# Another written order of all work, other engines for sums, scalings and divisions, and s and b loaded later, in a fused attention and two-layer MLP kernel

## The chip, the cores and the metric

One Trainium2 chip, one core. The time is in device microseconds (us) for one execution of the program. A run gives one time; the number compared is the median of several. The engines are PE (TensorE, matrix products), DVE (VectorE) and ACT (ScalarE), both elementwise, POOL (GpSimd, elementwise, works on SBUF alone) and SP (SyncE), which here only issues the DMA transfers. Each engine takes its instructions in order; DMA transfers are issued by SP in order too.

## What is computed

Windowed attention over 4 batches, 8 heads, 576 positions and head size 64, then two MLPs on the 2304 x 512 result, each 512 to 2048 to 512.

```python
scores = scale * q @ k.T                     # per head; scale = 1/8
scores = where((rel >= 0) & (rel < 128), scores - slope[h] * |rel|, -1e9)
attn = exp(scores - max); attn = attn / (sum(attn) + 1e-9)
x = (attn @ v) laid out as 2304 x 512
x = (s * relu(x @ w_in1)**2 + b) @ w_out1    # first MLP
out = relu(x @ w_in2)**2 @ w_out2            # second MLP
```

The MLP weights are fp64 words in memory.

## The kernel before

Every fp32 operand of the MLP products is split into a rounded half and the rest (hi and lo), and each product is made of three matmuls (hi by hi, hi by lo, lo by hi). A split is a copy on ScalarE (hi) followed by a subtraction on VectorE (lo) that waits for it. The fp64 weight words are turned to fp32 by a first stage (ScalarE scales the low words, VectorE merges), a second stage (a scaling, a shift on VectorE, an addition on GpSimd) and a split. Weights of the later parts are halved ahead of time, stored to DRAM and loaded again. Products of the later parts are made by seven instead of eight block products, for which sums and differences of weight blocks and of operands are made first.

All work is written out by hand as one order: the string `ORDER` (line 38 on) holds 2463 tokens, and line 1212 runs through it, each token calling one piece that issues instructions on one or more engines. The wrapper `InOrder` (line 19) keeps each engine's instructions in that order, SP's too. So the order of tokens is the order on every engine, and an instruction that waits holds up what is behind it on its own engine only. At most eight transfers are open at a time, since each takes one of eight semaphores in turn.

Tokens that matter here, k counting attention units, weight pieces or steps:

- `Dk`, `Sk`, `Pk`, `Tk`, `Ck`, `Uk`, `Xk` (lines 358 and 467): an attention unit's load, scores, probabilities (score, max and exp), divisions with transposes, copies out of PSUM, output products and their split into x (or, for the last blocks, a store to DRAM). Units 32 to 39 are the short blocks at the end of each batch (`tail_unit`, tiles with _t). `UNIT_ENGINES` says for units 0 to 31, six letters each, on which engine (s ScalarE, v VectorE) four divisions and two copies run.
- `lgi`, `agi`, `bgi`, `cgi` (line 278): load, first stage, second stage and split of piece i of weight group g of the first MLP. `PIECE_ENGINES` gives the engine of the scaling in b and of the subtraction in c.
- `Ln`, `Gn`, `Hn`, `Mn` (line 548): first product, relu and scaled square (needs s), shifted halves (needs b), second product of step n of the first MLP on attention blocks.
- `i` (line 711): loads s and b, each spread over the partitions, by two DMAs.
- `nk.i` (line 734): sums of first-MLP weight blocks, on GpSimd; `fk.i` their split and store; `kk.i` other stores.
- `lk.r`, `ak.r`, `bk.r`, `ck.i`, `dk.i`, `xk.r`, `yk.r`, `Sk.0`, `Sk.1`, `Nk.0`, `Nk.1`: the same for the second MLP's weights. `S` (line 864) makes sums of w_in2 blocks on VectorE, `N` (line 899) of w_out2 blocks on GpSimd, `R` and `t` split and store those.
- `wk.i` loads the weights of step k, `Yn.q` an input block, `Vn.m` and `Tn.i` split it and make its differences; `pk.m` are the first products of step k, `mk`, `uk`, `vk` copies out of PSUM, `jk.c`, `rk.c`, `hk.c` sum with relu, square and halves, `Fk.j` the second products.
- In the last two blocks `en.e` loads, `gn.e` makes the operand of, and `Xn.e` is second product e; `C` and `O` bring results out.

Of the kernel before, what the change touches and what calls it, by code (L numbers as in the profile page):

```python
# [15 lines left out]
P = 128  # L16


class InOrder:
# [19 lines left out]
    D0 S0 D3 D1 S3 l00 P0 S1 l02 P3 T0 i l03 P1 T3 T1 a02 C0 a00 U0 a03 b02 b00 D4 D2 S2 X0 D5 C1 P2 U1 S4 C3 P4 T2 T4  # L39
    U3 D6 l01 a01 c00 C2 U2 c02 b01 X3 X1 S5 X2 D7 L0 b03 l10 P5 L1 C4 T5 c01 G0 G1 c03 a10 L2 l12 L3 a12 l11 H0 C5 U4  # L40
    b10 H1 U5 G2 X4 X5 G3 a11 H2 c10 D8 b12 M0 M1 S7 S6 M2 l13 L4 L5 b11 H3 P7 P6 M3 T7 D9 T6 c11 C7 C6 l20 G4 U7 U6 L6
    G5 a13 H4 X6 c12 l22 G6 H5 L7 S8 M4 b13 P8 G7 X7 H6 M5 H7 L8 L9 T8 G8 L10 D10 l21 c13 G9 C8 U8 a20 H8 X8 a22 M6 L11
    S9 M7 G10 L12 M8 H9 b20 l23 P9 T9 G11 H10 b22 L13 H11 C9 U9 M9 D11 G12 G13 M10 X9 S10 L14 D12 M11 a21 a23 D13 H12
    L15 b21 P10 T10 M12 G14 H13 c21 c20 C10 M13 H14 U10 L16 G15 c22 l30 b23 X10 H15 G16 L17 l32 S11 L18 G17 L19 M14 M15
    P11 T11 H16 H17 c23 G18 a30 C11 k0.0 l31 G19 L20 U11 H18 k2.1 a32 X11 H19 G20 M16 S12 L21 M17 b30 M18 P12 T12 l33
    a31 G21 c30 M19 H20 C12 b31 U12 X12 L22 S13 a33 G22 L23 P13 M20 L24 T13 H21 b32 C13 H22 G23 c31 H23 G24 l34 M21 U13
    M22 c32 b33 H24 D14 l35 L25 X13 a34 G25 L26 G26 L27 c33 S14 L28 H25 H26 k5.0 D15 M23 M24 b34 P14 T14 G27 M25 C14 a35
    c34 U14 L29 b35 X14 G28 H27 H28 c35 L30 S15 G29 D16 k4.0 M26 P15 M27 M28 T15 C15 L31 H29 D17 G30 H30 U15 X15 M29 S16
# [112 lines left out]
def attention_mlp2_kernel(ctx, tc, first0, first1, qkv0, qkv1, qkvt, w_in1, w_out1, s_in, b_in, w_in2, w_out2, out):  # L165
# [1089 lines left out]
```

## Time and profile before

| | us |
|---|---|
| median of 3 runs | 930.66 |
| lowest run | 930.6 |
| the profiled execution, its own time | 926.7 |
| its span in the profile | 924.9 |
| PE busy in the span | 883.8 (96%) |
| DVE busy | 659.2 (71%) |
| ACT busy | 545.0 (59%) |
| POOL busy | 175.5 (19%) |

One run of the three took 2689.89 us; the median leaves it aside. Busy is the time in which an engine has an instruction at work. A PE instruction's end is modelled, since matmuls overlap, so PE busy is not PE at its peak. PEclk in the views is the clock that TensorE was granted, as a share of full speed. All lines of the kernel read L29, the wrapper, so instructions are told apart by tile names: `out<-in`. The tiles s, u are attention's PSUM banks, ha and oa the first MLP's, px, py, po and q the later products'; names that begin with m2 are places of later weights and operands, st the staging of weight words, sph and spl the weight sums and their halves, ywoh, ywol, yr and the like the results of squares in the last two blocks.

### The profile page before, as it was taken

The numbers are of one execution on the slowest core, as the hardware profiler recorded it, in microseconds if no ns is written. First come the engines' busy times: TensorE is split into PE (matmuls) and PEld (weight loads), VectorE is DVE, ScalarE is ACT, GpSimd is POOL, SyncE is SP. The second block draws the span as 40 slices with busy tenths as digits, with TensorE's granted clock in tenths as the row PEclk, the third lists the DMA queues.
The fourth block names the chain that finished last, engine by engine and source line by source line (L and its number), as shares of the span: only waits on it lengthen the run. The fifth ranks groups of instructions, "written<-read, shape, count | busy, mean of one in ns | idle before, by whom it ended". The sixth has DMA issues, their size and how long they took to land.

```text
span 924.9 us, 16342 instructions
## 1 busy us (share of the span) xinstructions
PE 883.8 (96%) x5680; PEld 790.0 (85%) x5680; DVE 659.2 (71%) x1471; ACT 545.0 (59%) x1242; POOL 175.5 (19%) x259
## 2 busy tenths in 40 slices
PE   5799999999999999889999999999999889999997
PEld 4689999877777787669999998888999879999987
DVE  6998886454446788756455876898858968648675
ACT  6988886444556578645444565766656535446442
POOL 3342231000026373300010012222243400000000
PEclk8999999999999999999999999999999999999999
DMA  8456525542229788979957958769899887867772
GB/s 317 168 158 178 185 90 171 160 140 65 75 63 307 245 274 269 316 279 358 313 192 263 365 178 283 267 214 318 306 342 339 306 289 254 267 258 239 245 241 80
DMA packets 131378, 216.83 MB, mean 234 GB/s; under 512 B 15840, under 2 KB 74208, under 8 KB 131296
## 3 DMA queue, kind: packets, MB, share of 16 engines
q1 hardware_dynamic: 131296, 215.79, 69.5%
q8 instruction: 45, 0.74, 0.3%
q14 instruction: 37, 0.30, 0.1%
HBM read 146.02 MB, written 69.73 MB: 233 GB/s over the span
## 4 chain that ended last, share of the span: by engine, by line
PE 75%; DMA 9%; DVE 6%; ACT 4%; issue 4%; POOL 2%; SPq 1%; ACTq 0%; DVEq 0%; POOLq 0%
PE px L29 13%; PE po L29 13%; PE oa L29 12%; PE ha L29 12%; PE py L29 10%; PE q L29 9%; PE s L29 6%; DMA m2wol<-wd 2%; POOL st L29 2%; PE u L29 1%; DMA st<-w_in 1%; SPq L29 1%; DMA raw<-first 1%; DMA xd<-raw_t 1%; DMA raw_t<-qkvt 1%
## 5 line engine op out<-in xcount | busy, mean ns | idle before, releaser
L29 POOL TENSOR_TENSOR st<-st 128x256 int32<-128x256 int32 (+1 forms) x120 | 83.9, 720 | 362.0 <-DVE st L29 297.2
L29 ACT ACTIVATE pr<-pr,nd 128x256 f32<-128x256 f32 (+1 forms) x129 | 59.5, 474 | 46.6 <-DVE nd L29 46.6
L29 ACT ACTIVATE st<-st 128x512 int32<-128x512 uint32 (+3 forms) x84 | 69.4, 840 | 4.9 <-DMA st<-w_out 3.0
L29 DVE SCALAR_TENSOR_TENSOR r_all<-r_all,s_sb 128x256 f32<-128x256 f32 (+1 forms) x64 | 42.2, 664 | 27.6 <-ACT r_all L29 27.5
L29 ACT ACTIVATE tr<-tr 128x384 f32<-128x384 f32 x48 | 25.3, 526 | 55.9 <-DVE tr L29 55.9
L29 PE MATMUL oa<-ga,woh 128*128 128x256 f32 x256 | 48.6, 289 | 0.0
L29 ACT ACTIVATE r_all<-ha 128x256 f32<-128x256 f32 (+1 forms) x64 | 30.7, 483 | 28.1 <-PE ha L29 26.3
L29 POOL TENSOR_TENSOR sph<-wih,wil 128x256 f32<-128x256 f32 x32 | 23.9, 772 | 121.3 <-PE ha L29 121.2
L29 DVE SCALAR_TENSOR_TENSOR st<-st 128x512 int32<-128x512 int32 (+1 forms) x42 | 38.0, 911 | 6.1 <-ACT st L29 5.7
L29 PEld LDWEIGHTS oa<-ga,woh 128*128 128x128 f32 x256 | 39.7, 191 | 2.8 <-issue 1.7
L29 DVE CUSTOM_DVE_ANT_0 pr<-s,bases 128x256 f32<-128x256 f32 (+1 forms) x96 | 31.7, 386 | 8.5 <-PE s L29 8.5
L29 PE MATMUL ha<-x0h,wih 128*128 128x256 f32 x128 | 37.6, 294 | 0.0
L29 PE MATMUL ha<-x0h,wil 128*128 128x256 f32 x128 | 36.3, 283 | 0.5 <-DVE wil L29 0.5
L29 PE MATMUL ha<-x0l,wih 128*128 128x256 f32 x128 | 36.2, 283 | 0.0
L29 PE MATMUL oa<-ga,wol 128*128 128x256 f32 x128 | 36.2, 283 | 0.0
L29 POOL TENSOR_TENSOR sph<-sph 128x256 f32<-128x256 f32 x32 | 27.1, 864 | 28.2 <-DVE spl L29 27.4
L29 PE MATMUL s<-raw 64*128 64x256 f32 (+1 forms) x224 | 29.6, 384 | 1.8 <-issue 1.8
L29 ACT ACTIVATE r_all<-px 128x384 f32<-128x384 f32 x32 | 15.6, 489 | 24.4 <-PE px L29 24.4
L29 PE MATMUL px<-m2xl,m2wil 128*128 128x384 f32 x138 | 27.8, 335 | 0.0
L29 DVE TENSOR_SCALAR st<-st 128x512 int32<-128x512 int32 (+1 forms) x42 | 22.8, 543 | 6.6 <-ACT st L29 6.1
L29 PEld LDWEIGHTS ha<-x0h,wih 128*128 128x128 f32 x128 | 24.4, 191 | 2.7 <-issue 2.0
L29 POOL TENSOR_TENSOR st<-st,st 128x256 f32<-128x256 f32 x24 | 22.3, 954 | 23.3 <-DMA st<-wx 20.9
(678 smaller groups left out, 2772.3 us busy)
## 6 DMA issues: line engine op xcount, KB each, us to landing
m2wih<-wd SPq DMA_DIRECT2D x19, 512.0 KB, 5.1
st<-w_in SPq DMA_DIRECT2D x8, 1024.0 KB, 6.6
st<-w_out SPq DMA_DIRECT2D x16, 512.0 KB, 4.6
ws<-spl SPq DMA_DIRECT2D x16, 512.0 KB, 5.4
m2wih<-ws SPq DMA_DIRECT2D x16, 512.0 KB, 6.7
wd<-m2wol SPq DMA_DIRECT2D x14, 512.0 KB, 5.7
m2wol<-we SPq DMA_DIRECT2D x26, 256.0 KB, 4.8
st<-w_out SPq DMA_DIRECT2D x6, 1024.0 KB, 7.2
```

The lines of the kernel that those rows point to most:

```text
L29: ins = op(*args, **kw)
```

## The change

`ORDER` has the same tokens in another sequence. Its beginning before and after:

```diff
-    D0 S0 D3 D1 S3 l00 P0 S1 l02 P3 T0 i l03 P1 T3 T1 a02 C0 a00 U0 a03 b02 b00 D4 D2 S2 X0 D5 C1 P2 U1 S4 C3 P4 T2 T4
-    U3 D6 l01 a01 c00 C2 U2 c02 b01 X3 X1 S5 X2 D7 L0 b03 l10 P5 L1 C4 T5 c01 G0 G1 c03 a10 L2 l12 L3 a12 l11 H0 C5 U4
+    D0 S0 D3 P0 S3 D1 l00 l02 P3 S1 T0 P1 T3 T1 a00 D4 D2 l03 C0 a02 b00 U0 X0 b02 S2 S4 C1 U1 C3 U3 P2 P4 T2 l01 D5 D6
+    T4 a03 a01 c00 b03 b01 C2 U2 D7 X1 S5 c02 X2 X3 L0 i l10 P5 L1 C4 T5 G0 c01 a10 C5 G1 U4 L2 c03 H0 b10 U5 l12 H1 L3
...
```

The end of the first MLP and the start of the second:

```diff
-    n7.3 T38 c1.3 n7.4 G61 w1.0 L62 d1.3 C38 X36 P39 U38 T39 w2.4 n7.5 w2.0 X38 c1.4 U37 x1.2 d1.4 H61 X37 c1.5 G62 C39
-    d1.5 M60 U39 L63 X39 Q Y0.0 M61 Y0.1 Y0.3 Y0.2 f7.0 w0.0 w0.1 H62 w0.3 G63 f7.1 M62 w1.1 V0.1 T0.1 H63 T0.3 M63 T0.2
...
+    c1.3 d1.3 X36 G61 C38 L62 U38 P39 w2.0 T39 x1.3 c1.4 x1.2 X38 n7.2 n7.3 H61 U37 M60 d1.4 C39 c1.5 X37 U39 d1.5 G62
+    X39 Q Y0.0 Y0.1 L63 n7.4 Y0.3 n7.5 M61 w0.0 Y0.2 w0.1 f7.1 H62 f7.0 G63 M62 V0.1 T0.1 H63 T0.2 w0.4 V0.5 M63 E40
...
```

Part of the second products of block 2:

```diff
-    p22.7 p22.5 e2.2 X2.0 v22 j22.1 y6.4 p22.3 j23.0 T3.2 r22.1 t4.2 N5.1 R5.2 X2.1 r23.0 R5.3 y6.5 N6.0 V3.1 p22.4 X2.2
-    R6.0 t4.3 p23.6 e2.5 V3.2 p23.5 R6.1 g2.6 g2.8 V3.6 t5.1 g2.7 j22.2 j22.3 r22.2 e2.3 X2.3 e2.4 r21.2 u23 r22.3 y7.4
-    X2.4 t5.0 g2.9 g2.10 X2.5 e2.7 N6.1 g2.11 p23.7 y7.5 R6.3 e2.10 v23 j23.1 e2.6 X2.6 t5.3 T3.4 r23.1 R6.2 r21.3 e2.9
...
+    R5.3 g2.6 g2.5 e2.9 g2.8 T3.4 X2.4 X2.5 X2.6 r22.3 V3.6 t6.1 g2.9 y7.5 g2.7 g2.10 N6.1 R6.3 g2.11 y7.4 w23.3 u23
+    g2.12 p23.7 N7.0 t6.0 v23 t5.0 t5.2 t5.3 e2.10 e2.13 j23.1 X2.7 X2.8 N7.1 r23.1 R7.2 p23.4 X2.9 R7.3 e2.11 g2.14
...
+    r23.3 g2.19 O2.2.2 g2.20 t6.3 O2.2.0 g2.21 X2.16 X2.17 X2.18 g2.24 X2.19 g2.22 t7.0 X2.20 g2.25 g2.26 X2.21 e2.27
+    e2.31 p24.2 m24 g2.27 g2.23 e2.35 X2.24 X2.25 X2.26 e2.23 X2.22 X2.27 g2.28 e2.30 e2.28 e2.40 e2.39 p24.6 g2.32
...
```

`UNIT_ENGINES` has other letters: 32 instead of 34 of the 128 divisions and 39 instead of 41 of the 64 copies are ScalarE's. A table by token, read by two helpers, chooses engines of the sums, of the scalings in b and of one subtraction in c; s and b become the two columns of one tile.

```diff
+CHOICE = dict(x.split(":") for x in """
+    N1.1:v N2.1:v N3.0:v N3.1:v N7.1:v S0.1:g S1.1:g S2.0:g S3.0:g S3.1:g S4.0:g b0.0:vg b2.2:vg b3.0:vg b3.1:vg
+    b33:vg b34:vg b4.1:vg b4.3:vg b5.2:vg b7.0:vg b7.2:vg c35:g n0.1:v n0.2:v n1.0:v n1.2:v n1.3:v n2.2:v n2.3:v
+    n3.1:v n4.3:v n4.5:v n5.1:v n5.4:v n6.1:v n6.2:v n7.1:v n7.2:v n7.3:v n7.5:v
+""".split())
...
-    s_sb = const.tile([P, 1], F32, tag="s_sb", name="s_sb")
-    b_sb = const.tile([P, 1], F32, tag="b_sb", name="b_sb")
+    sb = const.tile([P, 2], F32, tag="s_sb", name="s_sb")
+    s_sb, b_sb = sb[:, 0:1], sb[:, 1:2]
...
+    now = [""]
+
+    def choice(n, usual):
+        return CHOICE[now[0]][n] if now[0] in CHOICE else usual
+
+    def adder(usual):
+        return vector if choice(0, usual) == "v" else gpsimd
...
-        if engine == "s":
+        if choice(0, engine) == "s":
             scalar.activation(h, h, AF.Copy, scale=2.0 ** -112)
...
-        t, tt = pool_sum[0].bitcast(F32), gpsimd.tensor_tensor
+        t, tt = pool_sum[0].bitcast(F32), adder("g").tensor_tensor
...
-        (l0, l1, h0, h1), tt = quarters(k), vector.tensor_tensor
+        (l0, l1, h0, h1), tt = quarters(k), adder("v").tensor_tensor
...
-        lo, hi, tt = slice(0, BLK), slice(BLK, DM), gpsimd.tensor_tensor
+        lo, hi, tt = slice(0, BLK), slice(BLK, DM), adder("g").tensor_tensor
...
-    run(table[x] for x in ORDER.split())
+    for x in ORDER.split():
+        now[0] = x
+        table[x]()
```

Of the chosen tokens, `n` with a last digit under 4 makes one addition, with 4 or 5 two; `N` and `S` make two each; each `b` scales 128x512 words.

## Rows read from the trace of the kernel before

**Rows 1.** Page, busy us with share of the span and instructions.
```profile
PE 883.8 (96%) x5680; PEld 790.0 (85%) x5680; DVE 659.2 (71%) x1471; ACT 545.0 (59%) x1242; POOL 175.5 (19%) x259
```

**Rows 2.** Busy time by stretch: length, PE, PEld, DVE, ACT, POOL; PEclk; DMA share; GB/s.
```profile
0.00:75.00 75.00, 57.65 (x463) 49.01 (x464) 61.50 (x179) 60.49 (x142) 25.85 (x51) 0.93 0.64 220
75.00:350.00 275.00, 274.37 (x1846) 229.34 (x1846) 181.85 (x500) 171.75 (x437) 68.79 (x98) 1.00 0.51 161
350.00:400.00 50.00, 45.58 (x315) 35.70 (x316) 39.01 (x113) 36.60 (x98) 16.60 (x30) 1.00 0.89 293
400.00:425.00 25.00, 21.21 (x103) 18.41 (x102) 16.14 (x21) 11.97 (x22) 0.00 (x0) 0.93 0.87 305
425.00:700.00 275.00, 274.57 (x1471) 252.57 (x1471) 197.57 (x347) 159.22 (x320) 48.46 (x65) 1.00 0.81 282
700.00:775.00 75.00, 68.04 (x465) 64.68 (x465) 63.01 (x116) 36.67 (x83) 15.84 (x15) 1.00 0.85 287
775.00:850.00 75.00, 75.00 (x500) 75.00 (x499) 47.78 (x93) 39.36 (x83) 0.00 (x0) 1.00 0.79 273
850.00:924.90 74.90, 67.37 (x527) 65.24 (x525) 52.37 (x105) 28.93 (x62) 0.00 (x0) 1.00 0.60 189
```

**Rows 3.** Waits of PE, whole span: us in total, times, longest.
```profile
PE s L29 <- DMA rwih<-first: 4.2, 1, 4.2
PE s L29 <- DVE f_3woh L29: 4.0, 3, 2.2
PE s_t L29 <- DVE pr_t L29: 3.2, 5, 1.1
PE px L29 <- ACT tu L29: 2.7, 2, 2.1
PE q L29 <- DMA m2wol<-we: 1.4, 1, 1.4
```

**Rows 4.** Timeline of POOL and DVE, 728 to 768: start, us, operation, [idle before].
```profile
729.96 2.74 POOL L29 TENSOR_TENSOR st<-st,st 128x256 f32<-128x256 f32 x3 [1.74 <-DMA st<-wx]
...
731.02 1.08 DVE L29 TENSOR_TENSOR ywol<-ywol 128x384 f32<-128x384 f32 x1
...
736.92 0.55 DVE L29 TENSOR_TENSOR ywol<-ywol 128x384 f32<-128x384 f32 x1
```

**Rows 5.** The head: ACT's wait (5 to 35), then timeline rows of SP and PE.
```profile
ACT st L29 <- DMA st<-w_out: 2.5, 2, 1.8
...
3.15 0.47 SPq L29 DMA_DIRECT2D s_sb<-s_in  x1
...
19.48 1.65 PE L29 MATMUL s<-rwil 64*128 64x128 f32 x8 [3.17 <-DMA rwil<-first]
```

**Rows 6.** Timeline around 405: ACT, then PE.
```profile
404.85 0.84 ACT L29 ACTIVATE m2xh<-yf 128x768 fp32r<-128x768 f32 x1 [4.09 <-DMA yf<-xd]
...
406.36 0.49 PE L29 MATMUL oa<-ga_63h,woh 128*128 128x512 f32 x1 [1.31 <-ACT ga_63h L29]
408.75 0.50 PE L29 MATMUL oa<-ga_63l,woh 128*128 128x512 f32 x1 [1.90 <-DVE ga_63l L29]
```

**Rows 7.** Timeline of DVE and PE at 752, and DVE's last instruction.
```profile
752.66 0.56 DVE L29 TENSOR_TENSOR m2wih<-ywih,m2wih 128x384 fp32r<-128x384 f32 x1 [0.67 <-ACT m2wih L29]
...
752.68 1.69 PE L29 MATMUL q<-m2xl,m2wih 128*128 128x256 f32 x9 [1.09 <-ACT m2wih L29]
...
920.92 0.42 DVE L29 TENSOR_TENSOR ob<-q,k3u 128x256 f32<-128x256 f32 x1 [1.29 <-PE q L29]
```

**Rows 8.** Groups by shape, whole span: count, busy us, mean ns, idle before.
```profile
L29 POOL TENSOR_TENSOR sph<-wih,wil 128x256 f32<-128x256 f32 x32 | 23.9, 772 | 121.3 <-PE ha L29 121.2
...
L29 DVE TENSOR_TENSOR st<-st,st 128x256 f32<-128x256 f32 x12 | 5.4, 460 | 0.5
...
L29 ACT ACTIVATE st<-st 128x512 f32<-128x512 f32 x28 | 18.9, 674 | 1.5 <-DVE st L29 1.3
...
L29 DVE TENSOR_SCALAR st<-st 128x512 int32<-128x512 int32 x28 | 12.5, 445 | 5.1 <-ACT st L29 4.7
```

More of the change, by code (lines that the diff above doesn't have):

```diff
@@ L44 @@
[L44 to L48, printed above, removed]
@@ new lines @@
+    C11 G17 l32 a30 G18 U11 H17 X11 H18 L19 G19 b30 L20 S12 M16 L21 k0.1 a32 l31 M17 M18 P12 T12 a31 H19 G20 c30 C12 H20
+    L22 l33 G21 b32 U12 X12 L23 G22 H21 S13 L24 M19 a33 b31 M20 M21 H22 P13 l34 b33 T13 G23 C13 c31 a34 M22 H23 U13 L25
+    c33 G24 G25 c32 L26 k3.0 D14 L27 H24 M23 H25 X13 D15 S14 G26 G27 M24 l35 b34 L28 L29 P14 k4.1 T14 M25 H26 a35 C14
+    H27 c34 k4.0 G29 b35 U14 M26 D16 X14 G28 H28 S15 L30 c35 P15 M27 M28 T15 C15 D17 G30 L31 H29 G31 U15 X15 L32 S16 M29
+    H30 H31 D18 G32 L33 P16 T16 M30 D19 C16 H32 G33 M31 M32 H33 S17 U16 L34 P17 T17 X16 G34 C17 M33 L35 H34 S18 U17 M34
@@ new lines @@
+    F15.7 t0.0 R0.2 p17.2 F15.2 V2.3 F15.10 R0.3 t0.3 u16 t0.2 V2.5 p16.7 O1.1 y1.4 O1.4 v16 F15.8 y1.5 p17.1 w20.0
+    j16.0 F14.0 T2.4 p16.5 N1.0 V2.4 p16.4 Y3.0 m17 j17.0 j16.1 p16.3 r16.0 w19.2 j16.2 j16.3 r16.3 p17.5 y2.4 w19.1
+    p17.6 R1.0 N1.1 u17 F14.6 R1.1 p18.2 r17.0 y2.5 R1.2 t1.1 T3.1 t1.2 N2.0 p17.7 t1.0 F15.0 v17 j17.1 p18.1 m18 R1.3
+    p17.3 j17.3 w20.2 w20.1 t1.3 p18.6 O1.2 p17.4 u18 j18.0 w19.3 j17.2 N2.1 R2.1 p18.5 p18.7 R2.0 p19.1 v18 y3.4 t2.0
+    p18.4 r17.1 r17.3 R2.2 p19.2 R2.3 m19 y3.5 j18.1 j18.2 g2.0 w21.0 r18.0 p18.3 F15.6 p19.6 t2.2 j19.0 w20.3 j18.3
@@ new lines @@
+    e2.25 e2.19 C2.1.1 r23.2 g2.16 e2.20 e2.26 C2.1.0 e2.29 j23.3 X2.14 g2.17 e2.22 e2.21 g2.15 g2.18 X2.15 e2.24 p24.1
+    r23.3 g2.19 O2.2.2 g2.20 t6.3 O2.2.0 g2.21 X2.16 X2.17 X2.18 g2.24 X2.19 g2.22 t7.0 X2.20 g2.25 g2.26 X2.21 e2.27
+    e2.31 p24.2 m24 g2.27 g2.23 e2.35 X2.24 X2.25 X2.26 e2.23 X2.22 X2.27 g2.28 e2.30 e2.28 e2.40 e2.39 p24.6 g2.32
+    e2.32 X2.23 g2.33 C2.7.0 e2.33 X2.28 g2.29 X2.32 e2.36 g2.34 X2.33 X2.29 g2.30 e2.34 X2.34 g2.35 C2.7.1 e2.38 g2.31
+    X2.30 e2.47 w27.0 e2.37 e2.44 X2.35 e2.42 e2.43 X2.31 g2.36 e2.41 g2.40 g2.41 g2.37 g2.39 e2.46 X2.36 X2.40 C2.6.0
@@ new lines @@
+    X2.37 g2.38 e2.54 V3.4 u24 C2.6.1 e2.45 X2.38 e2.51 X2.39 X2.41 e2.49 g2.43 g2.46 g2.42 V3.7 g2.45 e2.48 O2.5.0
+    g2.44 X2.42 X2.43 X2.44 g2.47 X2.45 O2.5.2 p24.7 X2.46 g2.48 e2.53 V3.5 w25.0 v24 e2.50 X2.47 e2.52 g2.49 p24.4
+    w25.1 j24.0 p24.5 g2.50 O2.4.2 O2.4.0 X2.48 X2.49 g2.51 V3.3 w25.2 p25.1 j24.1 X2.50 X2.51 p24.3 e3.13 e2.55 p25.2
+    w26.0 j24.2 m25 w25.3 p25.6 w26.3 w27.1 g2.53 g2.52 X2.52 j24.3 u25 j25.0 w26.1 p25.5 p25.7 v25 X2.53 w26.2 w28.0
+    p26.1 j25.1 p25.4 p25.3 j25.2 w27.2 w28.1 p26.2 p27.1 w27.3 m26 j25.3 w28.2 w29.0 e3.12 g2.55 j26.0 p27.2 p26.6
@@ new lines @@
+    r29.2 j30.1 e3.1 r29.1 p31.2 w31.2 r30.0 r24.3 p30.3 m31 r28.3 j31.0 X3.0 e3.4 e3.3 p31.6 p30.4 j30.3 r30.1 r27.2
+    r30.3 g3.3 e3.8 e3.5 r29.3 e3.6 X3.1 r31.0 X3.2 u31 g3.10 g3.7 p31.7 p31.5 g3.6 e3.14 X3.3 X3.4 X3.5 e3.16 g3.12
+    e3.9 g3.11 v31 X3.6 p31.4 r26.1 e3.7 g3.8 e3.19 j30.2 j31.1 r30.2 e3.20 e3.52 X3.7 e3.15 X3.8 e3.18 e3.49 p31.3
+    r31.1 g3.13 e3.21 g3.14 g3.16 g3.9 X3.9 X3.10 X3.11 e3.17 g3.17 e3.22 j31.2 X3.12 r31.2 C3.1.0 g3.18 e3.50 g3.15
+    e3.26 C3.1.1 e3.23 g3.19 j31.3 X3.16 X3.17 X3.13 e3.24 g3.20 r31.3 e3.25 g3.27 X3.14 X3.18 X3.15 g3.24 g3.25 g3.21
@@ L267, in second_stage @@
         na, nw = words.shape[1:3]
-        da, dw = max(1, 2 * P // nw), min(nw, 2 * P)
+        eng, most = (gpsimd, 2 * P) if choice(1, "g") == "g" else (vector, DM)
+        da, dw = max(1, most // nw), min(nw, most)
         for i in range(0, na, da):
@@ L271, in second_stage @@
                 y = (slice(None), slice(i, i + da), slice(c, c + dw))
[L272 removed]
+                eng.tensor_tensor(to[y], h32[y], l32[y], ALU.add)
     last_load = []
@@ L308, in third @@
                 part = (slice(None), slice(n, n + step)) if k else (slice(None), slice(None), slice(n * P, (n + step) * P))
-                split(hi[part], lo[part], words()[..., 0].bitcast(F32), act_copy, pool_sub if how[1] == "g" else dve_sub)
+                split(hi[part], lo[part], words()[..., 0].bitcast(F32), act_copy, pool_sub if choice(0, how[1]) == "g" else dve_sub)
             how = PIECE_ENGINES[g][i]
@@ L541, in scaled_square @@
     def scaled_square(r):
[L542 removed]
+        vector.scalar_tensor_tensor(r, r, s_sb, r, ALU.mult, ALU.mult)
     def shifted_halves(hi, lo, r):
[L545 to L546 removed]
+        scalar.activation(hi, r, AF.Identity, bias=b_sb)
+        vector.scalar_tensor_tensor(lo, r, b_sb, hi.bitcast(F32), ALU.add, ALU.subtract)
     def step_of(n, d, f, lo, w, start, stop):
```

179 lines of the change are left out of this document (78 added, 101 removed).

## Prediction, made before the change was run

> **What bounds the kernel now.** I read the line of busy times first, then the busy time by stage, then TensorE's waits, and last the timelines of three places where TensorE stands still. The span is 924.9 us and TensorE is busy for 883.8 of it [rows 1]. So a change that leaves TensorE's work as it is, as this one does, has 41.1 us to win from. The stages [rows 2] say where: idle is the stretch less PE busy. It is 17.4 us in 0 to 75, 4.4 in 350 to 400, 3.8 in 400 to 425, 7.0 in 700 to 775 and 7.5 in 850 to the end. It is only 0.6 in 75 to 350, 0.4 in 425 to 700 and nothing in 775 to 850. In those last three stages (625 us) TensorE is the bound, and whatever VectorE, ScalarE and GpSimd do sooner there is not seen. Of the 41.1 some can't go: the first matmul stands for 4.2 us before its input has landed [rows 3], and about 4 us lie between the last eviction's start at 920.92, just behind the last matmul, and the end of the span [rows 7]. So some 33 us are open to an order, in four places.
>
> TensorE's own waits [rows 3] name VectorE and ScalarE more than DMA: three waits on f_3woh in the attention at the head, five on pr_t in the short attention blocks, two on tu, one on a loaded weight.
>
> **VectorE and GpSimd block each other.** The same VectorE subtraction of 128x384 takes 0.55 us at 736.92, with GpSimd idle, and 1.08 at 731.02, while three GpSimd sums run from 729.96 and take 2.74 together [rows 4]. The operation that comes second waits for the other's end. A consequence for this change: taking turns in the written order moves a wait from inside an instruction to in front of it. It makes the port no freer. Time comes back only where the delayed instruction was the one that TensorE stood for. The Trainium skill (SBUF — State Buffer, section Who interferes with whom) has a rule that speaks against a gain: a VectorE instruction with two SBUF inputs and a GpSimd instruction that reads SBUF exclude each other for the whole instruction, whoever starts first, so another sequence of the same pairs frees nothing. By that rule alone the term of 700 to 775 below would be 0 and the sum 926.7. The two rows agree with the exclusion; that the sequence can't matter to TensorE they do not show, so the term is made from the waits there.
>
> **The change, part by part.** The written order holds the same 2463 tokens; only their sequence differs, and each engine and the DMA queue follow it.
>
> *Engines of the sums.* 21 additions of the `n` tokens and 10 of the `N` tokens go from GpSimd to VectorE, 12 of the `S` tokens the other way. On GpSimd one takes 0.772 us, on VectorE 0.460 [rows 8]. VectorE: +31 x 0.46 - 12 x 0.46 = +8.7 us. GpSimd: -31 x 0.772 + 12 x 0.772 = -14.7. The piece of c35 goes to GpSimd (two additions, +1.5; about 0.7 less on VectorE). 11 scalings go from ScalarE, 0.674 each, to VectorE, 0.445 [rows 8]: -7.4 and +4.9. Of the divisions and evictions two each change to VectorE net, within 2 us. In all VectorE gets 13 to 15 us more, GpSimd 13 less, ScalarE some 8 less. VectorE has 93 us free of 275 in 75 to 350 (busy 181.85) and 77 of 275 in 425 to 700 [rows 2], where TensorE covers it: 0. In 350 to 400, where VectorE is busy for 39.0 of 50, about ten of the `n` sums land (4.6 us). Room is left, and the same sums stop blocking VectorE from GpSimd, so I put 0, with 2.5 either way. If that cover were gone, the price would be those 4.6.
>
> *s and b loaded later.* Their two loads, the first of them issued at 3.15, take about 0.47 us of issue each [rows 5], ahead of l03 and of the attention inputs. They go behind L0, where only G0 needs them, a product of 12 matmuls later. With them l03 (by the code 256 rows of 1024 words, 1 MB) is moved behind two attention inputs (D4 and D2, 0.5 and 0.4 MB), and l01 ahead of D5 and D6. D2 is what S2 stood 3.17 us for at 19.48 [rows 5]. By the 220 GB/s of 0 to 75 [rows 2] a megabyte takes 4.8 us, so D2 can come early enough for S2 not to wait for it. l03 comes later by D4 and D2, 0.9 MB or some 4 us, but its reader (a03) is moved behind two rounds of probabilities and T2.
>
> *The head.* ScalarE is what fills up there: it is busy 60.5 of 75, VectorE 61.5 [rows 2]. It waits 2.5 us for w_out [rows 5], because a02 and a03 stand ahead of work whose inputs are there. In the new order a00 comes first, whose words landed earlier, and a03 stands late, so these 2.5 can go. Of TensorE's waits at S2 and T2 (3.2 and up to 4.0 in three) more is named, but the same ScalarE work still stands ahead of L0. Hence I take the 2.5 and 0.5 of the small waits: **-3.0**. Bounds: -5.0 (S2's wait and half of the others gone) and +1.0 (l03 late for b03 and c03). TensorE is full from 75 on, so what is won here stays.
>
> *The switch of stages, 400 to 425.* ScalarE waits 4.09 us for a load of attention output (V0.1) at 404.85 and only then makes ga_63h, for which TensorE stands 1.31; VectorE then does V0.1 and T0.1 before ga_63l, for which TensorE stands 1.90 [rows 6]. In the new order V0.1 and T0.1 still precede H63, and TensorE still has L63, M61, M62 between U39 and M63. The wait must return: **0**, bounds -3 and +3. The granted clock is 0.93 here [rows 2], a mean of its two levels (2.4 and 1.2 GHz) right after those waits; that would return too.
>
> *700 to 775.* TensorE is idle 7.0 and VectorE busy for 63.0 of 75, GpSimd 15.8 [rows 2]. This is where blocking costs. The `N` sums that remain on GpSimd (N6, N7.0) sit among operands that TensorE needs; N7.1 moves to VectorE. Behind it, operands for the second products come singly, VectorE, then ScalarE, then VectorE again: at 752.66 VectorE waits 0.67 for ScalarE, and TensorE 1.09 [rows 7]. The new order lets p24.2 and p24.6 come sooner among these products and covers some of that. The wait on tu (2.1 of the 2.7) and half of the 1.09-type waits make **-3.0**. Bounds: -7.0, all idle gone; +3.0, if u23, now behind more operand copies on ScalarE, comes later still.
>
> *775 to the end.* Nothing of GpSimd is left there. 7.5 us idle less 4 after the last matmul leave 3.5; the order of operands alone differs: **-1.0**, from -3 to +2.
>
> Sum: -3.0 + 0 + 0 - 3.0 - 1.0 = -7.0. The profiled execution took 926.7 us around its span of 924.9, so 919.7; the median of the runs is 930.66, 4.0 above it, so **923.7 us**.
>
> **The rivals.**
> *Given back.* The head's 3 us vanish because VectorE and ScalarE are near full at 25 to 75, and in 700 to 775 transfers, at 0.85 of the DMA engines [rows 2], set the pace. For: PE waits on a DMA there [rows 3]. Against: most of those waits name ScalarE and VectorE. Time: 930.7 less 0 to 4, so 927 to 931.
> *Slower, by loads that come late.* One place: 425 to 700, where the DMA share is 0.81 [rows 2] and idle is 0.4 us only because each of about 16 steps (1471 matmuls, some 90 a step by the code) finds its weights. SP issues in order; a load placed behind a store whose VectorE half is late starts late. Price: one wait like the longest on a weight, 1.4 [rows 3], once or twice a step, 22 to 45 us, so 946 to 968. It outweighs the 7 us from five such waits on. Against: the loads of a step stand well ahead of its products in both orders.
> *Much faster, by the port.* If most of the 33 us hang on blocked instructions, the head's idle but for the first load (17.4 - 4.2 = 13.2) and the 7.0 of 700 to 775 go: 930.7 - 20.2 = 910.5. Against: at the head TensorE's longest waits are for loads, not for a blocked instruction [rows 3, 5].
>
> **How the numbers follow.** Forecast 0.55 (912 to 927), given back 0.25 (927 to 936 with its upper bounds), late loads 0.08 (of it 0.05 above 949.3), much faster 0.12 (below 912). About 2%, or 18.6 us, is what a measurement of this kernel can tell from no change: faster than 912.0 has 0.12, slower than 949.3 has 0.05, between them 0.83. The range 911 to 936 leaves out some 0.08 above and 0.12 below.
>
> **What would show it.** Right: S2 without its wait and the first product, L0, some 3 us sooner; both waits at M63 and the lowered clock still there; TensorE idle in the stretch that answers 700 to 775 near 4; VectorE busy some 13 us more less what blocking it lost. Wrong: waits on weights in the full stretches, or TensorE's idle total above 41.

## The result, and the profile after

The new kernel took 916.6 us in the median of four runs (914.44 to 919.35), against 930.63 for the kernel before beside it: a ratio of 0.986, 95% interval 0.983 to 0.988. A second measurement of it (below, e9) gave 917.81 against 928.77, 0.988 (0.986 to 0.990). The forecast was 923.7 with a range of 911 to 936, so the time lies inside the range, 7 us on the quick side of the forecast, and within the 2% that I gave 0.83. The profiled execution took 916.5 us (span 914.7), where that of before took 926.7.

First the page's line of busy times, to be read beside [rows 1]:

```profile
PE 878.5 (96%) x5680; PEld 787.4 (86%) x5680; DVE 663.4 (73%) x1504; ACT 536.7 (59%) x1227; POOL 167.7 (18%) x242
```

TensorE idles 914.7 - 878.5 = 36.2 us, before 41.1. Of the 10.2 us between the spans 4.9 are therefore idle time; 5.3 are busy time of the same 5680 matmuls. About half of these the granted clock explains (mean 0.996 instead of 0.993, 0.3% of 884 us); the rest I leave open, since a matmul's end is modelled. VectorE is busy 4.2 us more, ScalarE 8.3 less, GpSimd 7.8 less; I had forecast 13 more, 8 less and 13 less, and what became of the rest was not traced. The same stretches as in [rows 2], with the same columns:

```profile
0.00:75.00 75.00, 58.40 (x490) 50.08 (x492) 65.03 (x186) 63.25 (x146) 27.08 (x51) 0.95 0.69 237
75.00:350.00 275.00, 274.56 (x1855) 229.51 (x1854) 187.89 (x523) 170.36 (x442) 62.23 (x88) 1.00 0.51 162
350.00:400.00 50.00, 46.71 (x306) 36.74 (x304) 38.16 (x111) 32.87 (x86) 15.76 (x25) 1.00 0.87 280
400.00:425.00 25.00, 23.04 (x127) 20.97 (x128) 18.91 (x29) 14.44 (x26) 0.00 (x0) 1.00 0.89 325
425.00:700.00 275.00, 273.59 (x1466) 252.21 (x1465) 200.19 (x357) 155.03 (x314) 53.12 (x68) 1.00 0.82 288
700.00:775.00 75.00, 69.93 (x503) 67.20 (x502) 62.50 (x120) 41.52 (x92) 9.51 (x10) 1.00 0.85 288
```

The kernels stand at different work at the same time, so stretches of time can mislead when a kernel is 10 us ahead. For that reason I made a ledger by work. All kernels have the same matmuls. I gave each one the spacing at which matmuls of its shape follow each other undisturbed (229 ns for 128x512 and so on; 841 us in all) and read off when each kernel has done the same amount. A stage is then the time between two such marks; in the new kernel the marks 35, 300, 345, 360, 500, 550, 650 and 690 lie near 61, 341, 392, 412, 552, 604, 707 and 752 us. Each line is one profiled execution.

| us | to 35 (head) | 35-300 | 300-345 (short attention blocks) | 345-360 (switch) | 500-550 | 650-690 | all other | end |
|---|---|---|---|---|---|---|---|---|
| before | 64.6 | 280.5 | 54.1 | 21.1 | 51.1 | 49.2 | 399.8 | 920.5 |
| before, again (e5) | 66.9 | 280.6 | 53.9 | 21.0 | 51.1 | 49.3 | 399.9 | 922.6 |
| new | 61.4 | 279.8 | 51.2 | 19.6 | 51.7 | 45.1 | 401.5 | 910.3 |
| new, again (e9) | 61.4 | 279.8 | 51.1 | 19.0 | 51.8 | 45.3 | 400.8 | 909.1 |
| new order, old engines (e1) | 63.1 | 281.5 | 52.3 | 18.8 | 54.8 | 46.0 | 402.4 | 918.8 |
| old order, new engines (e2) | 69.5 | 284.8 | 53.5 | 22.3 | 52.5 | 49.3 | 402.2 | 934.1 |
| old units (e6) | 62.8 | 281.3 | 51.2 | 19.1 | 53.3 | 46.5 | 401.0 | 915.2 |
| old sums (e7) | 61.1 | 279.8 | 52.6 | 18.5 | 54.3 | 47.4 | 400.9 | 914.7 |

By means of the two pairs, 11.8 us went: 4.3 at the head, 0.7 in 35 to 300, 2.9 in the short attention blocks, 1.8 at the switch of stages, 4.1 in 650 to 690; 0.6 came back in 500 to 550 and 1.3 elsewhere, most of it behind 690. Outside the head and the switch, two executions of one kernel agree within 0.25 us in each named stage. Only 500 to 550 is less certain: the new kernel's order gives 51.7 there in four executions, but 52.9 and 52.6 in two variants (e8, e12) that differ from it elsewhere. And the mark 690 stands among waits of TensorE, so what lies on either side of it moves by a microsecond with the spacings taken: from 650 to the end together about 3 us went.

TensorE's waits, whole span, beside [rows 3] (us in total, times, longest):

```profile
PE s L29 <- ACT f_3woh L29: 4.5, 2, 2.8
PE s L29 <- DMA rwih<-first: 4.2, 1, 4.2
PE s L29 <- ACT f_3wol L29: 3.8, 1, 3.8
PE q L29 <- ACT m2woh L29: 2.3, 2, 1.5
PE oa L29 <- DVE ga_63l L29: 2.3, 1, 2.3
...
PE s_t L29 <- DVE pr_t L29: 1.7, 4, 0.7
...
PE px L29 <- ACT tr L29: 0.6, 1, 0.6
PE px L29 <- ACT tu L29: 0.6, 1, 0.6
```

S2's wait for rwil is gone (0.8 in e9), pr_t costs 1.7 instead of 3.2, tu 0.6 instead of 2.7. Two waits at the head took new names (f_3woh and f_3wol, both for ScalarE). At the switch one of the two waits of [rows 6] is left:

```profile
396.45 0.85 ACT L29 ACTIVATE m2xh<-yf 128x768 fp32r<-128x768 f32 x1 [2.98 <-DMA yf<-xd]
397.20 0.71 ACT L29 ACTIVATE ga_63h<-r_all,s_sb 128x512 fp32r<-128x512 f32 x1
...
400.81 0.50 PE L29 MATMUL oa<-ga_63l,woh 128*128 128x512 f32 x1 [2.30 <-DVE ga_63l L29]
```

ScalarE still stands for the load with ga_63h behind it, but 1.1 us less, and ga_63h is there when TensorE comes at 398.12.

### The profile page after: what moved, and what is told of

The parts are those of the page before. It is cut to its first block, busy times and chain, and to the rows that moved or that the text cites. A ratio compares the mean times of both kernels' runs of the same rounds, so it can differ in the third digit from the quotient of the medians.

```text
span 914.7 us, 16299 instructions
## 1 busy us (share of the span) xinstructions
PE 878.5 (96%) x5680; PEld 787.4 (86%) x5680; DVE 663.4 (73%) x1504; ACT 536.7 (59%) x1227; POOL 167.7 (18%) x242
## 4 chain that ended last, share of the span: by engine, by line
PE 81%; DVE 9%; ACT 4%; DMA 3%; issue 2%; SPq 1%; POOL 0%; ACTq 0%; DVEq 0%
PE ha L29 14%; PE po L29 14%; PE px L29 13%; PE oa L29 12%; PE py L29 10%; PE q L29 8%; PE s L29 7%; PE u L29 2%; DMA m2wol<-wd 1%; DVE ywoh L29 1%; DVE st L29 1%; DVE m2woh L29 1%; DVE pr_t L29 1%; DMA yf<-xd 1%; DMA st<-w_out 1%
## 5 line engine op out<-in xcount | busy, mean ns | idle before, releaser
L29 POOL TENSOR_TENSOR st<-st 128x256 int32<-128x256 int32 (+1 forms) x123 | 87.2, 729 | 363.8 <-DVE st L29 251.0
L29 ACT ACTIVATE st<-st 128x512 int32<-128x512 uint32 (+3 forms) x74 | 62.4, 859 | 5.6 <-DVE st L29 3.4
L29 PE MATMUL oa<-ga,wol 128*128 128x256 f32 x128 | 36.2, 283 | 0.0
L29 POOL TENSOR_TENSOR sph<-wih,wil 128x256 f32<-128x256 f32 x17 | 13.5, 814 | 117.7 <-PE ha L29 117.2
L29 DVE TENSOR_SCALAR st<-st 128x512 int32<-128x512 int32 (+2 forms) x52 | 26.2, 507 | 5.9 <-ACT st L29 5.1
L29 POOL TENSOR_TENSOR sph<-sph 128x256 f32<-128x256 f32 x26 | 22.6, 888 | 33.7 <-DVE spl L29 20.9
L29 PE MATMUL ha<-x2h,wih 128*128 128x512 f32 x64 | 26.4, 412 | 0.0
```

Source lines behind the costliest of these rows:

```text
L29: ins = op(*args, **kw)
```

## The experiments

Theory A of the place: the gain comes from which instruction stands ahead of which. Rival B, the port: it comes from the sums that left GpSimd and no longer block VectorE.

### Order and engines apart (e1, e2)

e1 keeps the new order and takes the old engines; e2 keeps the old order and takes the new engines.

```diff
 # e1: the new kernel, but
-CHOICE = dict(...the 41 choices...)
+CHOICE = {}
-UNIT_ENGINES = """vvvvss vvvvvs svvvsv vvvvss ...
+UNIT_ENGINES = """svvvvs vvvvss vvvvss vvvvsv ...
 # e2: the new kernel, but with ORDER of the kernel before
```

> The new written order with the old engines throughout (the table of choices empty, the old units). Theory A, place: what was gained (14 us of the median, 930.6 to 916.6) came from which instruction stands ahead of which at four places, and the choice of engines is worth 2 us either way. By it this kernel lies between 914 and 921 (ratio to the kernel before 0.983 to 0.990), L0 starts near 32.4 instead of 34.5, and M63 finds its gates without a wait on ScalarE. Rival B, port: at least half of the gain is that the sums moved from GpSimd to VectorE no longer block VectorE. By it the order alone gives 0 to 5 us, 925 to 931 (0.994 to 1.0), and the stretch that answers 700 to 775 keeps some 7 us of TensorE idle.

> The old written order with the new engines of sums, scalings, divisions and evictions. Theory A: 929 to 933 (ratio 0.998 to 1.002), every wait of the kernel before still there. Rival B: at least half of the 14 us, so 917 to 924 (0.985 to 0.993), with less idle on TensorE in 350 to 400 and 700 to 775. A third case: an engine chosen for one sequence is wrong in another, 934 or more.

Measured: e1 923.83 us, ratio 0.993 (0.991 to 0.995). e2 940.57 us, ratio 1.011 (1.009 to 1.013). The order alone gives 6 us, the engines alone cost 10, both together give 11 to 14. Neither theory holds as it was stated: A forecast e1 at 914 to 921 and e2 at no change, B forecast e2 at 917 to 924. The third case of e2 came true. The two halves can't be priced apart; the engines are worth -4 to -7 behind the new order, by its two measurements, and +10 behind the old one. Two of A's signs came in e1: L0 starts at 32.43, and TensorE has no wait on ScalarE at M63.

The ledger says where. The short attention blocks, the switch and 650 to 690 are quicker with the new order alone (52.3, 18.8, 46.0) and not with the engines alone (53.5, 22.3, 49.3), so there the order is the cause. In 650 to 690 that holds with a reserve: e1 gives back some 1.5 us behind 690, with a granted clock of 0.51 in 758 to 765. What the engines bring to the new order is to take back what it loses: 1.7 in 35 to 300 and 3.1 in 500 to 550, of which a part is again the clock (0.50 in 574 to 577, where the new kernel has 1.00). The 1.7 in the head can't be put down to them: L0 starts at 32.4 in both, and in e1's profile the clock is lower (0.85 in the first 30 us, against 0.96).

How engines chosen for another order cost time is seen in e2 at 305 (VectorE, then TensorE):

```profile
303.95 1.12 DVE L29 SCALAR_TENSOR_TENSOR r_all<-r_all,s_sb 128x512 f32<-128x512 f32 x1 [0.73 <-ACT r_all L29]
305.70 0.94 DVE L29 TENSOR_TENSOR sph<-wih,wil 128x256 f32<-128x256 f32 x1 [0.63 <-POOL sph L29]
306.56 0.41 DVE L29 CUSTOM_DVE_ANT_0 pr<-s,bases 128x256 f32<-128x256 f32 x1
...
309.55 1.14 DVE L29 TENSOR_SCALAR pr<-pr,nd 128x256 f32<-128x256 f32 x4
...
309.96 1.23 PE L29 MATMUL s<-ident,pr 128*128 128x128 f32 x8 [1.15 <-DVE pr L29]
```

An `n` sum that had been GpSimd's is now VectorE's. It stands where the old order had it, ahead of the probabilities pr. There it first waits 0.63 us for a place that GpSimd is still working on and then takes 0.94, beside three GpSimd sums. The pr chain starts some 1.6 us later for it, and TensorE stands 1.15 us for pr. On GpSimd the same sum had nothing behind it that TensorE wanted. The 0.46 us that the prediction wrote down for such a sum [rows 8] is the smaller part of the price; the rest is what the sum waits for, and who waits for it.

What the new order loses without its engines is seen in e1 at 568 to 573 (ScalarE, VectorE, TensorE), and what is left of it in the new kernel (last two lines, ScalarE and TensorE):

```profile
568.58 0.67 ACT L29 ACTIVATE st<-st 128x512 int32<-128x512 uint32 x1 [2.10 <-DMA st<-w_out]
569.27 0.69 DVE L29 SCALAR_TENSOR_TENSOR st<-st 128x512 int32<-128x512 int32 x1 [3.36 <-DMA wd<-m2wil]
572.58 1.32 PE L29 MATMUL px<-m2xh,m2wih 128*128 128x384 f32 x6 [2.03 <-ACT tr L29]
```
```profile
564.07 0.68 ACT L29 ACTIVATE st<-st 128x512 int32<-128x512 uint32 x1 [1.75 <-DMA st<-w_out]
567.30 1.31 PE L29 MATMUL px<-m2xh,m2wih 128*128 128x384 f32 x6 [0.60 <-ACT tr L29]
```

ScalarE stands for a weight piece whose load has not landed, and tr, which TensorE wants next, is queued behind it. The wait of TensorE is 2.0 in e1 and 0.6 in the new kernel. That is one place; what moved the rest of the 3.1 was not traced.

### Which engines (e6, e7)

e6 gives the new kernel the old units (divisions and copies of attention), e7 the old engines of all `n`, `N` and `S` sums.

```diff
 # e6
-UNIT_ENGINES = """vvvvss vvvvvs svvvsv vvvvss ...
+UNIT_ENGINES = """svvvvs vvvvss vvvvss vvvvsv ...
 # e7: left in CHOICE are b0.0 b2.2 b3.0 b3.1 b33 b34 b4.1 b4.3 b5.2 b7.0 b7.2 c35
-    N1.1:v N2.1:v N3.0:v N3.1:v N7.1:v S0.1:g S1.1:g S2.0:g S3.0:g S3.1:g S4.0:g
-    n0.1:v n0.2:v n1.0:v n1.2:v ...
```

> The new kernel with the old engines of divisions and evictions (its units); order and the 41 choices per token as in the new one. Order and old engines together gave 923.8, the new kernel 916.6: 7 us are the engines', in the new order. Theory E, an operand's engine sets when it is there: the units decide when f_3woh, tr and tu come, so at least half of the 7 are lost, 920 to 924 (ratio 0.989 to 0.993). Theory P, port: the units hardly touch what GpSimd does, so 916 to 918 (0.985 to 0.987).

> The new kernel with the old engines of all sums of the tokens n, N and S (31 back on GpSimd, 7 S tokens back on VectorE) and of c35 as new; order, units and scalings as in the new one. Theory P, port: the sums that block VectorE from GpSimd are what the engines' 7 us are, so 920 to 924 (0.989 to 0.993), with the loss in the stretches that hold them, 290 to 420 and 700 to 775. Theory E: 916 to 918.

e7 moves six `S` tokens back (12 additions), where its forecast says seven.

Measured: e6 920.39, ratio 0.991 (0.989 to 0.993); e7 921.13, ratio 0.991 (0.989 to 0.994). Against the new kernel's two measurements (0.986 and 0.988) e6 loses 2.5 to 5 us and e7 3 to 5.5, where e1, which loses both, has 4.5 to 7. So each theory's 920 to 924 came true and neither is singled out. The intervals touch those of the new kernel's second measurement, so the stages must speak: by the ledger the units are worth 1.5 in 35 to 300 (281.3, as in e1) and the sums 1.5 in the short attention blocks; in 650 to 690 the units are worth 1.3 and the sums 2.2, in 500 to 550, the less certain stage, about 1.5 and 2.5. They do not add up: e1, without both, loses 0.8 in 650 to 690. The price of 0 for two divisions and two copies net counted the wrong thing: the counts hardly change, but it matters which of them ScalarE does.

### The head (e3, e4, e8, e11)

e3 is the kernel before with the token `i` moved, e4 the kernel before with the new order up to L8 and the old one behind it.

```diff
 # e3
-    D0 S0 D3 D1 S3 l00 P0 S1 l02 P3 T0 i l03 P1 T3 T1 ...
+    D0 S0 D3 D1 S3 l00 P0 S1 l02 P3 T0 l03 P1 T3 T1 ...
-    ... X3 X1 S5 X2 D7 L0 b03 l10 ...
+    ... X3 X1 S5 X2 D7 L0 i b03 l10 ...
 # e4: ORDER = the new tokens up to L8, then the tokens left, in their old sequence
```

> The kernel before with one token moved: the loads of s and b are issued behind L0 instead of ahead of l03. Theory A: the two small loads cost 0.47 us of issue each and 1 us of transfer at most, S2 still waits for D2 behind l03, so at S2 1 us is won and 0 to 1 at the end: 929.5 to 931 (0.999 to 1.0). Rival C: the name of the change is its substance, and the late load of s and b is what takes S2's wait away: 927 to 928 (0.997).

> The kernel before, with the new order as far as L8 (work up to about 75 us), then the tokens that are left in their old sequence, old engines. Theory A: TensorE is full from 75 us on, so the 3.4 us that the new order has ahead by then stay to the end: 926.5 to 928 (0.995 to 0.997). Rival D, given back: ScalarE and VectorE or the loads behind it close the lead by 350 to 400: 930 to 931 (0.999 to 1.0).

Measured: e3 926.70, ratio 0.9964 (0.9949 to 0.9978); e4 926.24, ratio 0.9952 (0.9935 to 0.9969). The head's gain stays to the end, as theory A had it, against rival D. But all of it that can be told apart, 3.4 us of 3.8, is the late load of s and b: rival C. This rests on the medians. The profiles show less of it: by the ledger work 35 is done at about 65 us in e3 and 62.5 in e4, against 64.6 and 66.9 in the two of the kernel before. e3's profiled execution is its slowest (927.74), with a clock of 0.50 in 58 to 61.

Why two loads of 0.5 KB cost 3 us is seen at SP and in the transfer rate. First e5, the kernel before once more, then e3: SP's issues from S2's input on, the tenth load in e5 and the eighth in e3 (start, duration of the issue), then microseconds between 11 and 15 (last two columns: DMA share and GB/s) and the packets in 10 to 15.

```profile
6.75 0.46 SPq L29 DMA_DIRECT2D rwil<-first  x1
7.51 3.34 SPq L29 DMA_DIRECT2D raw<-first  x2
13.77 0.38 SPq L29 DMA_DIRECT2D st<-w_in  x1
...
11.00:12.00 1.00, 1.00 (x7) 0.78 (x6) 0.98 (x5) 0.61 (x4) 0.00 (x0) 1.00 0.88 152
12.00:13.00 1.00, 1.00 (x6) 0.78 (x4) 0.94 (x5) 0.00 (x0) 0.00 (x0) 1.00 0.51 164
13.00:14.00 1.00, 1.00 (x6) 0.72 (x4) 0.24 (x1) 0.23 (x1) 0.00 (x0) 1.00 0.61 246
14.00:15.00 1.00, 0.15 (x1) 0.00 (x0) 0.09 (x1) 1.00 (x2) 0.00 (x0) 1.00 0.64 250
...
DMA packets 552, 1.20 MB, mean 239 GB/s; under 512 B 260, under 2 KB 260, under 8 KB 552
```
```profile
4.21 1.49 SPq L29 DMA_DIRECT2D rwil<-first  x1
5.74 1.18 SPq L29 DMA_DIRECT2D raw<-first  x2
7.58 0.38 SPq L29 DMA_DIRECT2D st<-w_in  x1
10.61 2.17 SPq L29 DMA_DIRECT2D raw<-first  x1
13.20 0.68 SPq L29 DMA_DIRECT2D s_sb<-s_in  x1
...
12.00:13.00 1.00, 1.00 (x7) 0.94 (x6) 0.96 (x5) 0.00 (x0) 0.00 (x0) 1.00 1.05 430
13.00:14.00 1.00, 0.91 (x6) 0.67 (x4) 0.17 (x1) 0.79 (x1) 0.00 (x0) 1.00 0.99 406
...
DMA packets 549, 2.08 MB, mean 416 GB/s; under 512 B 36, under 2 KB 36, under 8 KB 549
```

At most eight loads are open, each on its semaphore, and in the traces the 9th to the 14th issue wait on those of the 1st to the 6th. In both kernels the 13th waits for the fifth, l02's 1 MB, and starts between 12.6 and 13.8. In e3 the twelve loads ahead of it are all large (384 KB to 1 MB), and the transfers run at 406 to 430 GB/s. In the kernel before two of the twelve are s and b. They hold two of the eight places for as long as a large load (10 us and more from issue to landing), but the places are not what they cost. They go in packets of 4 bytes, one for each partition. While these run (260 packets under 512 B in 10 to 15 us of e5, 36 in e3), the rate is 152 to 250 for four microseconds, although six large loads are open. In e8, which issues the two early as well (below), they hold their places from 4.2 and 5.4 on, also with six large loads open, and the rate in 9 to 13 is 394 to 425 all the same. It falls at 13 to 15, when their packets run (last line: 13 to 18):

```profile
13.00:14.00 1.00, 1.00 (x6) 0.82 (x5) 1.00 (x3) 1.00 (x3) 0.00 (x0) 1.00 0.85 143
14.00:15.00 1.00, 1.00 (x10) 0.76 (x10) 0.91 (x2) 1.00 (x2) 0.00 (x0) 1.00 0.52 129
...
DMA packets 636, 1.15 MB, mean 230 GB/s; under 512 B 293, under 2 KB 293, under 8 KB 635
```

In the head of these traces the loads land in the order of their issue. From the landing ahead of s to that of b it takes 3.2 us in e5 (13.75 to 16.93) and 1.8 in the first profile (12.61 to 14.43), where 512 KB take some 1.3, and the loads behind land later by it. S2's input lands at 21.76 in e5, at 19.44 in the first profile and at 18.02 in e3. That the packets are the reason is read from these times; no run changed them alone. TensorE's wait at S2:

```profile
21.81 1.65 PE L29 MATMUL s<-rwil 64*128 64x128 f32 x8 [3.74 <-DMA rwil<-first]
```
```profile
18.06 1.65 PE L29 MATMUL s<-rwil 64*128 64x128 f32 x8 [1.21 <-DMA rwil<-first]
```

The first is e5's, the second e3's.

e5 was run to see how much one profile of the kernel before tells:

> The kernel before once more, for a second profile: the first one was of an execution of 926.7 us, 3 to 4 below the median of its runs. If the terms of the sum rest on a lucky execution, this one shows another place with 2 to 4 us more TensorE idle, and which (the loads of the head, by its waits on rwih and rwil, or 700 to 775). If both profiles agree by stage within 0.5 us, the differences between runs lie outside the span.

Its profiled execution took 928.86, 2 us more than the first (926.7), and the whole difference is in the head (66.9 against 64.6 in the ledger): S2's input lands 2.3 us later. The clock is not the reason, since it is higher in e5 (0.98 in 0 to 75, against 0.93). Every other named stage agrees within 0.2. So the first profile was of an execution with a quick head.

e8 puts `i` back in the new kernel, ahead of l03 (behind D4 and D2):

```diff
-    ... T1 a00 D4 D2 l03 C0 a02 ...
+    ... T1 a00 D4 D2 i l03 C0 a02 ...
-    ... c02 X2 X3 L0 i l10 P5 ...
+    ... c02 X2 X3 L0 l10 P5 ...
```

> The new kernel with one token moved back: the loads of s and b are issued ahead of l03 again (here behind D2). Moving them alone gave 3.35 us in the kernel before, the whole new head 3.8. If the late load is the cause in the new order too, this one loses 2 to 4: 919 to 921 (ratio 0.987 to 0.990). If in the new order D4 and D2, which now stand ahead of them, are what counts, it loses 0 to 1: 916.6 to 917.6.

Measured: 917.81, ratio 0.988 (0.986 to 0.990). That is the new kernel's second measurement and 2 us above its first, so 0 to 2 us are lost, between the two cases. In the new order D2's load (rwil) is the seventh and goes ahead of the two small ones. S2 stands 0.8 for it in e8, and 0 and 0.8 in the two profiles of the new kernel; L0 starts at 33.88 instead of 32.4. Hence the 3.4 us of the late load can't be added to the rest of the new order: with `i` behind L0 in the old order, or with the new order and `i` early, most of S2's wait is gone (1.2 left in e3, 0.8 in e8).

e9 is the new kernel once more. e11 tries to win more at the head: C2 and U2 ahead of c00, and b03, b01 and c02 behind L0, since TensorE stands 3.78 for the copy C2.

```diff
-    T4 a03 a01 c00 b03 b01 C2 U2 D7 X1 S5 c02 X2 X3 L0 i l10 ...
+    T4 a03 a01 C2 U2 c00 D7 X1 S5 X2 X3 L0 b03 b01 c02 i l10 ...
```

> The new kernel once more, beside the three variants of it that follow, and for a second profile. 914.5 to 919 (ratio 0.983 to 0.988); by stage within 0.5 us of its first profile from 75 us on, the head within 2.5 by its loads.

> The new kernel with C2 and U2 ahead of c00, and b03, b01 and c02 behind L0. TensorE stands 3.78 us at 28.29 for f_3wol, whose eviction C2 stands on ScalarE behind 1.17 and 2.20 us of weights. Theory: L0 starts 2.5 to 3.5 us sooner (near 29.5) and, TensorE being full behind it, most of that stays: 913 to 914.5 (0.981 to 0.984). Rival D, given back: ScalarE does b03 and b01 anyway, L1 to G1 or l10 wait for it, and by 75 us nothing is left: 916 to 917.5.

Measured: e9 917.81, ratio 0.988 (0.986 to 0.990); e11 919.01, ratio 0.989 (0.988 to 0.991). L0 starts at 30.27 instead of 32.3, and that is given back by 39 us (work 15), where e11 is 0.7 us behind: rival D. What is late next, in e11 (VectorE, then TensorE):

```profile
29.78 0.70 DVE L29 TENSOR_SCALAR st<-st 128x1024 int32<-128x1024 int32 x1 [0.35 <-ACT st L29]
30.83 0.91 DVE L29 TENSOR_SCALAR st<-st 128x1024 int32<-128x1024 int32 x1 [0.35 <-ACT st L29]
31.89 1.40 DVE L29 TENSOR_TENSOR wol<-st,woh 128x1024 fp32r<-128x1024 f32 x1 [0.15 <-ACT woh L29]
...
36.82 1.23 PE L29 MATMUL s<-ident,f_0wih 128*128 128x128 f32 x8 [2.25 <-DVE f_0wih L29]
```

The weight pieces that C2 no longer waits for now stand on VectorE ahead of the next probabilities (f_0wih), and TensorE stands 2.25 us there.

### The switch (e10, e12)

e10 moves H63 ahead of V0.1 and T0.1 in the new kernel; e12 does that and e11's move.

```diff
-    ... G63 M62 V0.1 T0.1 H63 T0.2 w0.4 V0.5 M63 ...
+    ... G63 M62 H63 V0.1 T0.1 T0.2 w0.4 V0.5 M63 ...
```

> The new kernel with one token moved: H63 ahead of V0.1 and T0.1, so that neither ScalarE nor VectorE stands for the load of attention output with the last gate behind it. If V0.1 and T0.1 ahead of H63 are what TensorE stands for at M63 (2.30 us on ga_63l), that wait goes and the first product p0.1 starts 2 us sooner: 913.5 to 915.5 (0.983 to 0.985). Rival: p0.1 needs what V0.1 makes from the same late load, so the wait moves there: 916 to 917 (0.9855), and p0.1 starts at 403.5 as now.

> Both of the moves, H63 ahead of V0.1 and C2 early. The two places are 370 us apart with TensorE full between them, so the gains add: 911 to 913.5 (0.979 to 0.982) if both hold, else what the one that holds gives.

Measured: e10 917.99, ratio 0.988 (0.987 to 0.990); e12 921.15, ratio 0.991 (0.988 to 0.993). TensorE in e10, and the stretch 405 to 410 with the columns of [rows 2]:

```profile
404.48 1.31 PE L29 MATMUL px<-m2xh,m2wol 128*128 128x384 f32 x6 [1.16 <-DMA m2wol<-ws]
406.44 0.44 PE L29 MATMUL py<-m2xl,m2wol 128*128 128x384 f32 x1 [0.65 <-ACT m2xl L29]
407.43 1.86 PE L29 MATMUL py<-m2xl,m2wol 128*128 128x384 f32 x5 [0.55 <-DVE m2xl L29]
...
405.00:410.00 5.00, 3.81 (x14) 3.22 (x13) 3.43 (x6) 2.69 (x4) 0.00 (x0) 0.76 1.04 418
```

The 2.30 us for ga_63l are gone, so V0.1 and T0.1 are what TensorE stood for. But the first products of the next stage now wait for their weights and for their input, 2.4 us in three places (the new kernel waits at the last of them alone, 0.56), and the granted clock is 0.76 in 405 to 410, where the new kernel has 1.00. So the switch takes 20.5 instead of 19.0 and 19.6. That is the rival, with the clock on top of it. e12 is slower than either move alone, so nothing adds up: in its profile the first product waits 2.3 for its weights, and the clock is 0.53 in 405 to 410. None of the three variants beats the new kernel.

## Why the prediction was right, and where not

**The head, -3.0: right in size, wrong in its reason.** The ledger has -4.3, the medians of e4 have -3.8. I took 2.5 of the 3.0 from ScalarE's wait for w_out and priced s and b at two issues of 0.47. e3 shows that their late load alone is worth 3.4 in the old order. The step that failed is the price of a small load by its issue time: what the two cost is the 1.8 to 3.2 us by which the loads behind them land later. S2 without its wait and L0 earlier, which I had named as signs, both came (L0 32.4 instead of 34.5).

**Engines of the sums, 0: wrong.** The argument was that VectorE has room in 75 to 350 and that TensorE covers it. e2 shows +10 for the choices behind the old order, e1 against the new kernel -4 to -7 behind the new one. Busy share was the wrong measure: VectorE's room is not where the sum stands, and what counts is what is queued behind the sum.

**The short attention blocks, 0: missed.** 2.9 us went there (pr_t waits 1.7 instead of 3.2). The prediction looked only at the sums that land there, not at the order around the blocks; e1 shows 1.7 of it by order alone.

**The switch, 0 with both waits to return: half wrong.** The wait on ga_63l is there at 2.30, the one on ga_63h is not, and the lowered clock (0.93) did not return (1.00). The token sequence V0.1, T0.1, H63 is the same, as I read, but ScalarE's wait for the load before it fell from 4.09 to 2.98. SP asks for it at 401.44 in the kernel before, 3.6 us before TensorE comes to ga_63h, and at 392.99 in the new one, 5.1 before. So a wait for a load depends on when the load was asked for, not only on the sequence of its readers. 1.8 us, inside the bound of 3.

**700 to 775, -3.0: right.** 4.1 us went between work 650 and 690 by the ledger, and idle of TensorE in the stretch is 5.1 instead of 7.0 (I had asked for near 4). Behind 690 about 1 came back, so from 650 to the end some 3 went, where I had 4 in the two terms. The wait on tu of 2.1, from which the term was made, is gone from this stage (0.4 in e9). The Trainium skill (SBUF — State Buffer, section Who interferes with whom) has a VectorE instruction with two SBUF inputs and a GpSimd instruction that reads SBUF exclude each other, and I had drawn from it that another sequence of the same pairs frees nothing, hence a term of 0. The exclusion agrees with [rows 4] (0.55 us alone, 1.08 beside GpSimd sums); the conclusion, which was mine, fails. e1 keeps the old engines, changes the sequence alone, and wins 3.2 of the 4.1, and about 1.5 of the 3 to the end.

**775 to the end, -1.0: wrong in sign, small.** It took about 1.0 more by the ledger, with the reserve on the mark 690.

**425 to 700, 0.** About 1 us came back there, by a wait of 0.6 on tr and others like it behind loads that land late. This is the mechanism of my slower rival, but in one or two steps instead of all sixteen.

The sum of -7.0 against 11.8 in the ledger is short by the two zeros at 300 to 360 (4.7); the other differences cancel (head -1.3, 35 to 300 -0.7, 650 to 690 -1.1, against +0.9 in 425 to 700 and +2.0 at the end). For the profiled execution I had 919.7, and the two of the new kernel took 916.5 and 915.3: 3 to 4 us of the error. The other 3 come from the 4.0 that I added to reach the median: that was for the most part the quick head of before's first profile (2.3), and the new kernel's profiled executions lie only 0.1 and 2.5 below its medians.

By runs instead of stages: the order alone (e1) gives 6.2 of the 7.0 that I had, all of it put down to the order, and the engines, put at 0, give another 4 to 7 behind the new order. So the forecast was near for the order, but with the head's reason wrong, two stages missed and losses elsewhere that cancel their gain: that the sum fits is partly luck. What it lacked is the engines' term, which by e2 has no price of its own apart from the order.

## What to carry to other kernels

In a kernel with one written order, an instruction's engine and its place are one decision: price a move by what stands behind the instruction on its new queue and by what it waits for there, not by that engine's idle share. A load's price at the start is the time by which the loads behind it land later, and neither its issue nor its bytes tell it: two loads of 0.5 KB in packets of 4 bytes took as much of it as some 0.7 to 1.2 MB in large ones (1.8 to 3.2 us, at 1.3 for 512 KB). So small loads that nobody needs yet go behind the large ones. And when one wait is taken away in a stage where several engines are nearly full, look for the next one in line before counting the gain.

## What was not expected of the hardware

The head's time depends on the granted clock as well as on the order. The new kernel's first 30 us hold 118 matmuls in 15.11 us of busy time at a mean clock of 0.96; e10, with the same order up to there, takes 18.15 us for 120 at 0.81 (the two levels are 1.2 and 2.4 GHz), and is 2.3 us later at work 35 although TensorE has idled 2.6 us less in the first 75. The clock is not all of it: of the two profiles of the kernel before, the one with the higher clock in the head is 2.3 us slower there, by its loads (e5). Two executions of one kernel differ by 2 to 3 us by either cause, so one profile can't tell variants of the head apart below that.

Nor is a fall of the clock tied to one wait's length. It fell to half behind a wait of 2.03 us in e1 (572.58) and behind one of 2.32 in e12 (404.88), but stayed at 1.00 behind 2.30 in the new kernel (400.81). What decides it no run here settles.
